# Wider load runs, a new token order and a new step order in a fused attention and channel-mix kernel

## The chip, the cores and the metric

The kernel runs on one core of one Trainium2 chip. The metric is the device time of one launch in microseconds (us), lower is better. The kernel before takes 303.88 us (median of 2 runs). Its profiled execution has a span of 301.2 us; about 2 us of launch lie between span and time. Where I speak of "fast" and "slow" runs: a run is slow when it is more than 1.5% above the fastest of its kernel, and such runs are left out.

## The reference

Eight batches of 576 tokens with 8 heads of 64. Heads 0 to 3 attend to the last 32 tokens ("plain"). Heads 4 to 7 attend to every fourth of the last 128 ("dilated"). The result is the input of a channel mix: interpolation with the token before, two matrix products with a squared ReLU between, and a sigmoid gate.

```python
mask_plain = (rel >= 0) & (rel < 32)
mask_dil   = (rel >= 0) & (rel < 128) & (rel % 4 == 0)
attn = softmax(where(mask, q @ k.T / 8, -1e9)) @ v            # (8, 8, 576, 64)
x = attn.transpose(0, 2, 1, 3).reshape(8, 576, 512)
xk, xr = mu_k * x + (1 - mu_k) * x_prev, mu_r * x + (1 - mu_r) * x_prev
out = sigmoid(xr @ w_r) * (maximum(xk @ w_k, 0)**2 @ w_v)     # (8, 576, 512), float32
```

## The kernel before

One batch's attention is cut into steps: T (transposes of q and k on TensorE, evacuated by ScalarE into `QKp` and `QKd`), S (scores, exponential, mask: `AT`), P (the product with v, then a reciprocal and a product on VectorE: `x`), X (transposes of x) and the interpolation ("lerp": `dx`, `md`, `xk`, `xr`). The channel mix ("MoE" in the code) runs in nine tiles of 512 tokens; a tile has 20 groups of 4 matmuls (8 of K, then R and V). The next batch's attention steps are placed between these groups. Engines execute in program order.

```python
    def load_qk(b, sc):                       # one token per partition, one head = 256 B
        ...
            nc.gpsimd.dma_start(out=t[:ns, w].rearrange("p (h d) -> p h d", h=H),
                                in_=src[b].transpose([1, 0, 2])[r0:r0 + ns])
    ...
    make_identity(nc, ident)
    ...
    load_batch(0)
    ...
    load_batch(1)
    ...                                       # then the loads of wk, wr, wv

    def step_T(b, sc):                        # 8 transposes of 128 columns, five such steps a batch
        ...
        nc.scalar.activation(out=QKp[b % 2][:, :, PAD + r0:PAD + r0 + ns], in_=tb[:, 0:4, 0:ns], func=AF.Copy)
        nj = ns // R
        o = QKd[b % 2][:, :, PAD:].rearrange("p a (r j) -> p a r j", r=R)[:, :, :, r0 // R:r0 // R + nj]
        nc.scalar.activation(out=o, in_=tb[:, 4:8, 0:ns].rearrange("p a (j r) -> p a r j", r=R), func=AF.Copy)
    ...
    def step_K(tt, f):
        ...
        nc.scalar.activation(out=kr, in_=pk, func=AF.Relu, scale=8.0)
        nc.vector.tensor_tensor(out=k2_of[tt][:, f], in0=kr, in1=kr, op=ALU.mult)
    ...
        for i in range(NB):                   # attn_plan: what follows which MoE group
            at(2 * i, lambda i=i: step_S(b, i))
            at(2 * i + 2, lambda i=i: step_P(b, i, 0))
            at(2 * i + 3, lambda i=i: step_P(b, i, 1))
            at(2 * i + 4, lambda i=i: step_X(b, i))
        at(15, lambda: step_lerp_d(b))
        at(16, lambda: step_lerp(b, 0))
        at(18, lambda: step_lerp(b, 1))
        ...                                   # step_T(b + 1, sc) at 4 * sc + 1
        for tt in range(NTT):
            if tt + 2 < B:
                load_batch(tt + 2)
            plan = attn_plan(tt + 1)
            for g, f in enumerate(moe_groups(tt)):
                f()
                for a in plan.get(g, []):
                    a()
```

`tb`, the PSUM tile behind T and X, has one buffer.

The softmax here doesn't subtract the row's maximum and nothing guards it: scores larger than these inputs give would overflow.

## Time and profile before

The page of the kernel before shows busy tenths in 40 slices of 7.5 us:

```profile
span 301.2 us, 5488 instructions
PE 234.5 (78%) x2000; PEld 123.6 (41%) x2000; DVE 195.0 (65%) x520; ACT 163.1 (54%) x333; POOL 160.1 (53%) x227
PE   1413553598998899789978987898889789999993
DMA  9999999999999999959995999581101201202222
q0 software_dynamic: 126336, 18.10, 86.9%
```

The DMA row looks like a bound for 200 us. But a busy queue bounds only if someone waits for it. TensorE's timeline (start, us, operation, count, and in brackets its idle time before and what ended that) says where tiles begin; these are the first K matmuls of tiles 0, 1, 2 and 5:

```profile
53.80 1.86 PE L249 MATMUL mm<-xk,wk 128*128 128x512 f16 x4 [3.50 <-DVE xk L237]
87.52 1.02 PE L249 MATMUL mm<-xk,wk 128*128 128x512 f16 x4 [0.26 <-DVE xk L237]
116.85 1.02 PE L249 MATMUL mm<-xk,wk 128*128 128x512 f16 x4 [0.54 <-DVE xk L237]
205.61 1.03 PE L249 MATMUL mm<-xk,wk 128*128 128x512 f16 x4
```

All nine: 53.8, 87.5, 116.9, 147.0, 176.2, 205.6, 234.5, 261.8, 279.2. Tiles take about 29.4 us whether loads are under way or not (the tile from 205.6 has almost none: 28.9), and 17.4 us without attention. What TensorE waits for inside a tile, from the same view:

```profile
154.92 0.26 PE L207 MATMUL tb<-ident,x_2058 96*128 96x96 f16 x2 [0.61 <-DVE x_2058 L195]
158.30 0.33 PE L207 MATMUL tb<-ident,x_2110 96*128 96x96 f16 x4 [0.31 <-ACT QKd_94 L159]
181.43 0.30 PE L188 MATMUL xo<-VA_96,AT_97 128*128 128x65 f16 x4 [1.62 <-DVE AT_97 L180]
```

No load is among them. Waits for loads are at the start only: 5.0 and 1.1 us for batch 0 itself, 8.1 and 1.2 us for batch 1's q and k near 24 us, 2.2 us for batch 2's near 60.

### The profile page before, as it was taken

How to read it: one execution, taken by the hardware profiler on the slowest of the kernel's cores; microseconds unless marked ns; L12 is line 12 of the kernel's file. 1: busy time of each engine (PE TensorE's matmuls, PEld its weight loads, DVE VectorE, ACT ScalarE, POOL GpSimd, SP SyncE). 2: the span in 40 equal slices, each digit the busy share in tenths (PEclk: the TensorE clock that was granted, in tenths of full speed). 3: DMA queues.
4: the chain of work that ended last, by engine and by line, in shares of the span. 5: the costliest groups of instructions: out<-in, count | busy, mean ns of one | idle time of the engine just before them, and what ended most of it. 6: DMA issues, size and time to landing. Idle time of an engine off the chain costs nothing.

```text
span 301.2 us, 5488 instructions
## 1 busy us (share of the span) xinstructions
PE 234.5 (78%) x2000; PEld 123.6 (41%) x2000; DVE 195.0 (65%) x520; ACT 163.1 (54%) x333; POOL 160.1 (53%) x227
## 2 busy tenths in 40 slices
PE   1413553598998899789978987898889789999993
PEld 0302342145444454445445434544454344444441
DVE  2007545946598669866986697669766976872421
ACT  1512553267647754675477557756874475352530
POOL 8999995989989999457744774440000000000000
PEclk9999999999999999999999999999999999999998
DMA  9999999999999999959995999581101201202222
GB/s 65 123 71 112 102 92 203 178 111 72 147 172 115 144 134 140 129 37 115 162 89 38 114 153 98 37 113 39 33 24 50 70 2 35 70 37 77 64 57 85
DMA packets 133052, 27.91 MB, mean 93 GB/s; under 512 B 126368, under 2 KB 127904, under 8 KB 133024
## 3 DMA queue, kind: packets, MB, share of 16 engines
q0 software_dynamic: 126336, 18.10, 86.9%
q1 hardware_dynamic: 6688, 9.45, 10.4%
q8 instruction: 16, 0.26, 0.4%
q14 instruction: 12, 0.10, 0.1%
HBM read 36.18 MB, written 9.44 MB: 151 GB/s over the span
## 4 chain that ended last, share of the span: by engine, by line
PE 32%; DVE 12%; ACT 5%; issue 2%; DVEq 0%
PE mm L269 11%; PE mm L249 9%; PE mm L258 4%; DVE md L229 3%; PE tb L207 2%; ACT kr L252 2%; PE ps L171 2%; PE xo L188 2%; DVE ot L273 2%; DVE xk L237 1%; DVE xr L237 1%; ACT QKd_94 L159 1%; PE tb L154 1%; ACT QKp_92 L156 1%; DVE AT_97 L180 1%
## 5 line engine op out<-in xcount | busy, mean ns | idle before, releaser
L249 PE MATMUL mm<-xk,wk 128*128 128x512 f16 x288 | 74.2, 390 | 5.2 <-DVE xk L237 5.2
L252 ACT ACTIVATE kr<-mm 128x512 f16<-128x512 f32 x72 | 42.7, 597 | 38.3 <-PE mm L249 30.3
L261 ACT ACTIVATE sg<-mm 128x512 f32<-128x512 f32 x36 | 21.5, 598 | 32.0 <-PE mm L258 16.5
L249 PEld LDWEIGHTS <-wk 128*128 128x128 f16 x288 | 25.2, 99 | 31.8 <-issue 4.2
L258 PE MATMUL mm<-wr,xr 128*128 128x512 f16 x144 | 37.0, 379 | 0.0
L273 DVE SCALAR_TENSOR_TENSOR ot<-sg,mm 128x512 f32<-128x512 f32 x36 | 24.6, 684 | 19.0 <-PE mm L269 19.0
L210 ACT ACTIVATE xT<-tb 128x192 f16<-128x192 f16 x48 | 15.9, 331 | 20.9 <-PE tb L207 20.9
L83 POOL DMA_DIRECT2D VA_96<-in_v_dram x36 | 23.5, 657 | 6.1 <-PE xo L188 5.6
L83 POOL DMA_DIRECT2D VA_95<-in_v_dram x36 | 24.5, 701 | 4.1 <-PE xo L188 3.2
L77 POOL DMA_DIRECT2D VA_96<-in_v_dram x24 | 18.0, 752 | 15.6 <-PE ps L171 13.9
L77 POOL DMA_DIRECT2D VA_95<-in_v_dram x24 | 18.9, 788 | 9.1 <-PE ps L171 7.5
L229 DVE TENSOR_SCALAR md<-dx,mu 128x576 f16<-128x576 f16 x64 | 22.6, 414 | 0.0
L156 ACT ACTIVATE QKp_92<-tb 128x512 f16<-128x512 f16 (+1 forms) x20 | 11.1, 552 | 18.5 <-PE tb L154 18.5
L156 ACT ACTIVATE QKp_91<-tb 128x512 f16<-128x512 f16 (+1 forms) x20 | 11.1, 553 | 17.4 <-PE tb L154 17.4
L258 PEld LDWEIGHTS <-xr 128*128 128x128 f16 x144 | 12.7, 98 | 12.6
L219 DVE TENSOR_TENSOR dx<-xT 128x1728 f16<-128x1728 f16 x8 | 8.5, 1058 | 11.9 <-ACT xT L212 11.9
L212 ACT ACTIVATE xT<-tb 128x192 f16<-128x192 f16 x48 | 15.6, 324 | 0.0
L177 ACT ACTIVATE AT_98<-ps 128x768 f16<-128x768 f32 x16 | 13.0, 814 | 4.3 <-PE ps L171 4.1
L188 PEld LDWEIGHTS <-AT_97 128*128 128x128 f16 x128 | 7.5, 103 | 18.1 <-DVE AT_97 L180 12.8
L180 DVE TENSOR_TENSOR AT_99<-AT_99,mk_177 128x768 f16<-128x768 f16 x16 | 8.9, 558 | 8.3 <-ACT AT_99 L177 8.3
L128 DVE COPY mk_168<-m_153 128x96 f16<-128x96 f16 x8 | 1.6, 400 | 19.6 <-POOL m_153 L116 19.6
L180 DVE TENSOR_TENSOR AT_98<-AT_98,mk_168 128x768 f16<-128x768 f16 x16 | 8.9, 557 | 6.7 <-ACT AT_98 L177 6.7
(532 smaller groups left out, 529.9 us busy)
## 6 DMA issues: line engine op xcount, KB each, us to landing
out_dram<-ot SPq DMA_DIRECT2D x8, 256.0 KB, 2.4
VA_95<-in_v_dram POOLq DMA_DIRECT2D x28, 64.0 KB, 3.1
VA_96<-in_v_dram POOLq DMA_DIRECT2D x28, 64.0 KB, 3.1
out_dram<-ot SPq DMA_DIRECT2D x8, 224.0 KB, 2.4
out_dram<-ot SPq DMA_DIRECT2D x8, 192.0 KB, 2.4
out_dram<-ot SPq DMA_DIRECT2D x8, 160.0 KB, 2.5
wk<-in_moe_w_k_dram POOLq DMA_DIRECT2D x4, 256.0 KB, 6.1
wv<-in_moe_w_v_dram POOLq DMA_DIRECT2D x8, 128.0 KB, 4.9
```

The lines of the kernel that those rows point to most:

```text
L77: nc.gpsimd.dma_start(out=va[row:128, i, 0:4, 0:D], in_=v[b].transpose([1, 0, 2])[lo:hi, 0:4, :])
L83: nc.gpsimd.dma_start(out=va[row:row + n, i, 4:8, 0:D], in_=vr[r, j:j + n, 4:8, :])
L156: nc.scalar.activation(out=QKp[b % 2][:, :, PAD + r0:PAD + r0 + ns], in_=tb[:, 0:4, 0:ns], func=AF.Copy)
L180: nc.vector.tensor_tensor(out=at[:, :, :, 0:QB], in0=at[:, :, :, 0:QB], in1=MK[combos[i]], op=ALU.mult)
L210: nc.scalar.activation(out=xT[:, 0:2].rearrange("p c (r j) -> p c r j", r=R)[:, :, :, nj * i:nj * (i + 1)], in_=tb[:, 0:2, 0:QB].rearrange ...
L229: nc.vector.tensor_scalar(out=md[:, c], in0=dx[:, c], scalar1=mu[:, w, c:c + 1], scalar2=None, op0=ALU.mult)
L249: nc.tensor.matmul(out=pk, lhsT=wk[:, c, f * 128:(f + 1) * 128], rhs=xk_t[tt][:, c], start=(c == 0), stop=(c == 3))
L252: nc.scalar.activation(out=kr, in_=pk, func=AF.Relu, scale=8.0)
L258: nc.tensor.matmul(out=pr, lhsT=xr_t[tt][:, c, ts * 128:(ts + 1) * 128], rhs=wr[:, c], start=(c == 0), stop=(c == 3))
L261: nc.scalar.activation(out=sg, in_=pr, func=AF.Tanh, scale=0.5)
L269: nc.tensor.matmul(out=pv, lhsT=k2_of[tt][:, f, ts * 128:(ts + 1) * 128], rhs=wv[:, f], start=(f == 0), stop=(f == 7))
L273: nc.vector.scalar_tensor_tensor(out=ot, in0=sg_of.pop((tt, ts)), scalar=1.0, in1=pv, op0=ALU.add, op1=ALU.mult)
```

## The change

Its intent is fewer and longer DMA runs. q and k come in 1-KB runs of four tokens per partition (512 B once cast to fp16); dilated v in 512-B runs; the 32 v rows that neighbouring blocks share are copied by VectorE (`fix_v`) instead of loaded twice. This changes the token order, so T makes 96 small transposes instead of 40. Weights are loaded ahead of batch 1, and tile 0 is run without waiting for batch 1. The core of the diff:

```diff
+            nc.gpsimd.dma_start(out=t[:nj, w], in_=src[b].rearrange("h (j r) d -> j h (r d)", r=R)[j0:j0 + nj])
 ...
+    load_batch(0)
     make_identity(nc, ident)
 ...
-    load_batch(1)
     ...                                      # loads of wk, wr, wv
+    load_batch(1)
 ...                                          # step_T, plain heads: 8 blocks, 96 or 48 columns each
+                    for par in range(2):
+                        nc.tensor.transpose(out=tv[par * D:(par + 1) * D, wi, sl, :],
+                                            in_=t[:nj, w, 2 * hp + par, r * D:(r + 1) * D], identity=ident[:nj, :nj])
+                o = QKp[b % 2][:, w, :, PAD:].rearrange("p h (j r) -> p h r j", r=R)[:, :, :, j0:j0 + nj]
+                nc.scalar.activation(out=o, in_=tv[:, wi].rearrange("p (h r) x -> p h r x", h=2), func=AF.Copy)
 ...                                          # step_X for two blocks at once; md as one two-tensor product
+            for n, g in enumerate((5, 9, 13, 15, 17, 18)):
+                at(g, lambda n=n: step_T(b + 1, n))
+            at(19, lambda: fix_v(b + 1))
 ...
-        plan = attn_plan(0)                  # with T of batch 1 in it
-        for g in range(20): ...
+        for i in range(NB):
+            step_S(0, i); step_P(0, i, 0); step_P(0, i, 1)      # X after every second i
+        ...
+            if tt == 0:
+                plan = {}
 ...                                          # tile 0 alone, then:
+            if tt == 0:
+                for n in range(6):
+                    step_T(1, n)
+                fix_v(1)
+                plan = attn_plan(1)          # attention 1 alone
```

More of the change, by code (lines that the diff above doesn't have):

```diff
@@ L41 @@
     const = ctx.enter_context(tc.tile_pool(name="const", bufs=1))
-    ldp = ctx.enter_context(tc.tile_pool(name="ldp", bufs=10))
+    ldp = ctx.enter_context(tc.tile_pool(name="ldp", bufs=4))
     xp = ctx.enter_context(tc.tile_pool(name="xp", bufs=2))
     xtp = ctx.enter_context(tc.tile_pool(name="xtp", bufs=2))
-    lerp_p = ctx.enter_context(tc.tile_pool(name="lerp_p", bufs=2))
+    lerp_p = ctx.enter_context(tc.tile_pool(name="lerp_p", bufs=1))
     xkp = ctx.enter_context(tc.tile_pool(name="xkp", bufs=3))
@@ L53 @@
     p_tb = ctx.enter_context(tc.tile_pool(name="p_tb", bufs=1, space=PS))
-    QKp = [const.tile([128, 4, PAD + S], FP16, name=f"QKp{i}") for i in range(2)]
-    QKd = [const.tile([128, 4, PAD + S], FP16, name=f"QKd{i}") for i in range(2)]
-    VA = [const.tile([128, NB, H, D + 1], FP16, name=f"VA{i}") for i in range(2)]
+    QKp = [const.tile([128, 2, 2, PAD + S], FP16, name=f"QKp{i}") for i in range(2)]
+    QKd = [const.tile([128, 2, 4, PAD + S // 2], FP16, name=f"QKd{i}") for i in range(2)]
@@ L59, with load_qk @@
+    VAp = [const.tile([128, NB, 4, D + 1], FP16, name=f"VAp{i}") for i in range(2)]
+    VAd = [const.tile([128, NB // 2, 4 * (2 * D + 1) + 1], FP16, name=f"VAd{i}") for i in range(2)]
     AT = [const.tile([128, 2, 4, 128], FP16, name=f"AT{i}") for i in range(3)]
+    JC = ((0, 96), (96, 48))
     ld = {}
-    def load_qk(b, sc):
-        ns = min(128, S - sc * 128)
-        r0 = sc * 128
-        t = ldp.tile([128, 2, DM], FP16, name="qk16")
+    def load_qk(b, jc):
+        j0, nj = JC[jc]
+        t = ldp.tile([96, 2, H, R * D], FP16, name="qk16")
@@ L67, in load_qk @@
         for w, src in ((0, q), (1, k)):
-            nc.gpsimd.dma_start(out=t[:ns, w].rearrange("p (h d) -> p h d", h=H),
-                                in_=src[b].transpose([1, 0, 2])[r0:r0 + ns])
-        ld[(b, sc)] = t
-    def load_v(b, i):
-        va = VA[b % 2]
-        lo = max(0, QB * i - PAD)
-        hi = QB * (i + 1)
-        row = lo - (QB * i - PAD)
-        nc.gpsimd.dma_start(out=va[row:128, i, 0:4, 0:D], in_=v[b].transpose([1, 0, 2])[lo:hi, 0:4, :])
-        vr = v[b].rearrange("h (j r) d -> r j h d", r=R)
-        while lo < hi:
-            r, j = divmod(lo, J)
-            n = min(hi - lo, J - j)
-            row = lo - (QB * i - PAD)
-            nc.gpsimd.dma_start(out=va[row:row + n, i, 4:8, 0:D], in_=vr[r, j:j + n, 4:8, :])
-            lo += n
+            nc.gpsimd.dma_start(out=t[:nj, w], in_=src[b].rearrange("h (j r) d -> j h (r d)", r=R)[j0:j0 + nj])
@@ new lines, in load_qk, with load_v @@
+        ld[(b, jc)] = t
+    def load_v(b):
+        vp, vd = VAp[b % 2], VAd[b % 2]
+        for h in range(4):
+            nc.gpsimd.dma_start(out=vp[PAD:128, :, h, 0:D], in_=v[b, h].rearrange("(i p) d -> p i d", p=QB))
+        vr = v[b, 4:8].rearrange("h (j a r) d -> a j h (r d)", a=2, r=2)
+        for i in range(3):
+            lo, hi = QB * i, QB * (i + 1)
+            while lo < hi:
+                a, j = divmod(lo, J)
+                n = min(hi - lo, J - j)
+                row = PAD + lo - QB * i
+                nc.gpsimd.dma_start(
+                    out=vd[row:row + n, i, 1:].rearrange("p (h x) -> p h x", h=4)[:, :, 0:2 * D],
+                    in_=vr[a, j:j + n])
+                lo += n
@@ L86, in load_batch, with fix_v @@
+    def fix_v(b):
+        vp, vd = VAp[b % 2], VAd[b % 2]
+        nc.vector.tensor_copy(out=vp[0:PAD, 1:NB].rearrange("p i h x -> p i (h x)"),
+                              in_=vp[QB:128, 0:NB - 1].rearrange("p i h x -> p i (h x)"))
+        nc.vector.tensor_copy(out=vd[0:PAD, 1:3], in_=vd[QB:128, 0:2])
     def load_batch(b):
-        for sc in range(5):
-            load_qk(b, sc)
-        for i in range(NB):
-            load_v(b, i)
+        for jc in range(2):
+            load_qk(b, jc)
+        load_v(b)
@@ L92 @@
     ident = const.tile([128, 128], FP16)
+    load_batch(0)
     make_identity(nc, ident)
     for i in range(2):
-        nc.vector.memset(QKp[i][:, :, 0:PAD], 0.0)
-        nc.vector.memset(QKd[i][:, :, 0:PAD], 0.0)
-        nc.vector.memset(VA[i][0:PAD, 0], 0.0)
-        nc.vector.memset(VA[i][:, :, :, D:D + 1], 1.0)
+        nc.vector.memset(QKp[i][:, :, :, 0:PAD], 0.0)
+        nc.vector.memset(QKd[i][:, :, :, 0:PAD], 0.0)
+        nc.vector.memset(VAp[i][0:PAD, 0], 0.0)
+        nc.vector.memset(VAd[i][0:PAD, 0], 0.0)
+        nc.vector.memset(VAp[i][:, :, :, D:D + 1], 1.0)
+        nc.vector.memset(VAd[i][:, :, 0:4 * (2 * D + 1) + 1:2 * D + 1], 1.0)
@@ L99 @@
     for i in range(3):
         nc.vector.memset(AT[i][:, :, :, QB:128], 0.0)
-    load_batch(0)
     wk = const.tile([128, 4, DFF], FP16, name="wk")
@@ L109 @@
     nc.vector.tensor_scalar(out=mu, in0=mu, scalar1=-1.0, scalar2=None, op0=ALU.add)
+    ones = const.tile([128, S], FP16, name="ones")
+    nc.vector.memset(ones, 1.0)
+    murep = const.tile([128, 2, 4, S], FP16, name="murep")
+    for w in range(2):
+        for c in range(4):
+            nc.scalar.activation(out=murep[:, w, c], in_=ones, func=AF.Copy, scale=mu[:, w, c:c + 1])
     m01 = const.tile([128, 3, QB], FP16, name="m01")
@@ L123 @@
     MK = {}
-    for combo in ((START, START), (FULL, MID), (FULL, FULL), (FULL, START)):
+    for combo in ((START, START), (FULL, START), (FULL, MID), (FULL, FULL)):
         t = const.tile([128, 2, 4, QB], FP16, name=f"mk{combo[0]}{combo[1]}")
@@ L129 @@
         MK[combo] = t
-    combos = [(START, START), (FULL, MID), (FULL, FULL), (FULL, START), (FULL, MID), (FULL, FULL)]
-    load_batch(1)
+    combos = [(START, START), (FULL, START), (FULL, MID), (FULL, MID), (FULL, FULL), (FULL, FULL)]
     for c in range(4):
@@ L142, in scale_wv @@
             nc.vector.tensor_scalar(out=wv[:, c], in0=wv[:, c], scalar1=1.0 / 128.0, scalar2=None, op0=ALU.mult)
-    def step_T(b, sc):
-        ns = min(128, S - sc * 128)
-        r0 = sc * 128
-        t = ld.pop((b, sc))
-        tb = p_tb.tile([128, 8, 128], FP16, name="tb")
-        for g in range(2):
-            for w in range(2):
-                for hp in range(2):
-                    c = g * 2 + hp
-                    nc.tensor.transpose(out=tb[:, g * 4 + w * 2 + hp, 0:ns],
-                                        in_=t[:ns, w, c * 128:(c + 1) * 128], identity=ident[:ns, :ns])
-        nc.scalar.activation(out=QKp[b % 2][:, :, PAD + r0:PAD + r0 + ns], in_=tb[:, 0:4, 0:ns], func=AF.Copy)
-        nj = ns // R
-        o = QKd[b % 2][:, :, PAD:].rearrange("p a (r j) -> p a r j", r=R)[:, :, :, r0 // R:r0 // R + nj]
-        nc.scalar.activation(out=o, in_=tb[:, 4:8, 0:ns].rearrange("p a (j r) -> p a r j", r=R), func=AF.Copy)
+    T_STEPS = ((0, 0, 0), (0, 0, 1), (0, 1, 0), (0, 1, 1), (1, 0, None), (1, 1, None))
@@ new lines, in step_T @@
+    def step_T(b, n):
+        jc, g, w1 = T_STEPS[n]
+        j0, nj = JC[jc]
+        t = ld[(b, jc)]
+        tb = p_tb.tile([128, 768], FP16, name="tb")
+        ws = (0, 1) if w1 is None else (w1,)
+        nw = len(ws)
+        tv = tb.rearrange("p (w s x) -> p w s x", w=nw, s=8)
+        for wi, w in enumerate(ws):
+            for sl in range(8):
+                if g == 0:
+                    hp, r = sl // 4, sl % 4
+                    for par in range(2):
+                        nc.tensor.transpose(out=tv[par * D:(par + 1) * D, wi, sl, :],
+                                            in_=t[:nj, w, 2 * hp + par, r * D:(r + 1) * D], identity=ident[:nj, :nj])
+                else:
+                    h, rp = sl // 2, sl % 2
+                    nc.tensor.transpose(out=tv[:, wi, sl, :], in_=t[:nj, w, 4 + h, rp * 2 * D:(rp + 1) * 2 * D],
+                                        identity=ident[:nj, :nj])
+        if g == 0:
+            for wi, w in enumerate(ws):
+                o = QKp[b % 2][:, w, :, PAD:].rearrange("p h (j r) -> p h r j", r=R)[:, :, :, j0:j0 + nj]
+                nc.scalar.activation(out=o, in_=tv[:, wi].rearrange("p (h r) x -> p h r x", h=2), func=AF.Copy)
+        else:
+            for wi, w in enumerate(ws):
+                o = QKd[b % 2][:, w, :, PAD:].rearrange("p h (a j) -> p h a j", a=2)[:, :, :, j0:j0 + nj]
+                nc.scalar.activation(out=o, in_=tv[:, wi].rearrange("p (h a) x -> p h a x", h=4), func=AF.Copy)
@@ L166, in step_S @@
         for sl in range(4):
-            g, hp = sl // 2, sl % 2
-            QK = (QKp, QKd)[g][b % 2]
             for par in range(2):
                 ho = par * 64
-                nc.tensor.matmul(out=ps[:, par, sl * QB:(sl + 1) * QB],
-                                 lhsT=QK[ho:ho + 64, 2 + hp, QB * i:QB * i + 128],
-                                 rhs=QK[ho:ho + 64, hp, PAD + QB * i:PAD + QB * (i + 1)],
-                                 start=True, stop=True)
+                if sl < 2:
+                    lhsT = QKp[b % 2][ho:ho + 64, 1, sl, QB * i:QB * i + 128]
+                    rhs = QKp[b % 2][ho:ho + 64, 0, sl, PAD + QB * i:PAD + QB * (i + 1)]
+                else:
+                    h, ii = 2 * (i % 2) + sl - 2, i // 2
+                    lhsT = QKd[b % 2][ho:ho + 64, 1, h, QB * ii:QB * ii + 128]
+                    rhs = QKd[b % 2][ho:ho + 64, 0, h, PAD + QB * ii:PAD + QB * (ii + 1)]
+                nc.tensor.matmul(out=ps[:, par, sl * QB:(sl + 1) * QB], lhsT=lhsT, rhs=rhs, start=True, stop=True)
         at = AT[at_n[0] % 3]
@@ L184, in step_P, with step_X @@
         at = at_of[(b, i)]
-        va = VA[b % 2]
-        xo = p_xo.tile([128, 4, D + 1], FP32, name="xo")
-        for hl in range(4):
-            nc.tensor.matmul(out=xo[:, hl], lhsT=at[:, hl % 2, g * 2 + hl // 2, :], rhs=va[:, i, g * 4 + hl, :],
-                             start=True, stop=True)
         rec = xp.tile([128, 4], FP32, name=f"rec{g}")
-        nc.vector.reciprocal(out=rec[:QB], in_=xo[:QB, :, D])
+        x16 = xp.tile([128, 4, D], FP16, name=f"x16{g}", bufs=4)
+        xo_of[(b, i, g)] = x16
         if g == 0:
-            xo_of[(b, i)] = xp.tile([128, H, D], FP16, name="x16")
-        x16 = xo_of[(b, i)]
-        nc.vector.tensor_tensor(out=x16[:QB, g * 4:g * 4 + 4, :], in0=xo[:QB, :, 0:D],
-                                in1=rec[:QB].unsqueeze(2).to_broadcast([QB, 4, D]), op=ALU.mult)
+            xo = p_xo.tile([128, 4, D + 1], FP32, name="xo")
+            for hl in range(4):
+                nc.tensor.matmul(out=xo[:, hl], lhsT=at[:, hl % 2, hl // 2, :], rhs=VAp[b % 2][:, i, hl, :],
+                                 start=True, stop=True)
+            nc.vector.reciprocal(out=rec[:QB], in_=xo[:QB, :, D])
+            nc.vector.tensor_tensor(out=x16[:QB], in0=xo[:QB, :, 0:D],
+                                    in1=rec[:QB].unsqueeze(2).to_broadcast([QB, 4, D]), op=ALU.mult)
+        else:
+            xo = p_xo.tile([128, 2, 2 * D + 2], FP32, name="xo")
+            for hl in range(2):
+                for par in range(2):
+                    o = (2 * (i % 2) + hl) * (2 * D + 1) + par * (D + 1)
+                    nc.tensor.matmul(out=xo[:, hl, par * (D + 1):(par + 1) * (D + 1)], lhsT=at[:, par, 2 + hl, :],
+                                     rhs=VAd[b % 2][:, i // 2, o:o + D + 1], start=True, stop=True)
+            rv = rec.rearrange("p (h a) -> p h a", h=2)
+            nc.vector.reciprocal(out=rv[:QB], in_=xo[:QB, :, 0:2 * D + 2:2 * D + 1])
+            nc.vector.tensor_tensor(out=x16[:QB].rearrange("p (a h) d -> p h a d", a=2),
+                                    in0=xo[:QB, :, 1:2 * D + 1].rearrange("p h (a d) -> p h a d", a=2),
+                                    in1=rv[:QB].unsqueeze(3).to_broadcast([QB, 2, 2, D]), op=ALU.mult)
     xT_of = {}
-    def step_X(b, i):
-        x16 = xo_of.pop((b, i))
+    def step_X(b, ii):
         if b not in xT_of:
@@ L204, in step_X @@
         xT = xT_of[b]
-        tb = p_tb.tile([128, 8, 128], FP16, name="tb")
-        for c in range(4):
-            nc.tensor.transpose(out=tb[:, c, 0:QB], in_=x16[:QB].rearrange("p h d -> p (h d)")[:, c * 128:(c + 1) * 128],
-                                identity=ident[:QB, :QB])
-        nj = QB // R
-        nc.scalar.activation(out=xT[:, 0:2].rearrange("p c (r j) -> p c r j", r=R)[:, :, :, nj * i:nj * (i + 1)],
-                             in_=tb[:, 0:2, 0:QB].rearrange("p c (j r) -> p c r j", r=R), func=AF.Copy)
-        nc.scalar.activation(out=xT[:, 2:4, QB * i:QB * (i + 1)], in_=tb[:, 2:4, 0:QB], func=AF.Copy)
+        tb = p_tb.tile([128, 768], FP16, name="tb")
+        tv = tb.rearrange("p (g c x) -> p g c x", g=2, c=2)
+        for u in range(2):
+            x0 = xo_of.pop((b, 2 * ii + u, 0)).rearrange("p h d -> p (h d)")
+            x1 = xo_of.pop((b, 2 * ii + u, 1)).rearrange("p h d -> p (h d)")
+            for c in range(2):
+                nc.tensor.transpose(out=tv[:, 0, c, u * QB:(u + 1) * QB], in_=x0[:QB, c * 128:(c + 1) * 128],
+                                    identity=ident[:QB, :QB])
+                nc.tensor.transpose(out=tv[:, 1, u, c * QB:(c + 1) * QB], in_=x1[:QB, c * 128:(c + 1) * 128],
+                                    identity=ident[:QB, :QB])
+        nj = 2 * QB // R
+        nc.scalar.activation(out=xT[:, 0:2].rearrange("p c (r j) -> p c r j", r=R)[:, :, :, nj * ii:nj * (ii + 1)],
+                             in_=tv[:, 0].rearrange("p c (j r) -> p c r j", r=R), func=AF.Copy)
+        lo, hi = QB * ii, QB * (ii + 1)
+        while lo < hi:
+            a, j = divmod(lo, J)
+            n = min(hi - lo, J - j)
+            o = lo - QB * ii
+            nc.scalar.activation(
+                out=xT[:, 2:4].rearrange("p c (a r j) -> p c a r j", a=2, r=2)[:, :, a, :, j:j + n],
+                in_=tv[:, 1].rearrange("p c (r x) -> p c r x", r=2)[:, :, :, o:o + n], func=AF.Copy)
+            lo += n
     xk_t, xr_t = {}, {}
@@ L227, in step_lerp @@
         md = lerp_p.tile([128, 4, S], FP16, name="md")
-        for c in range(4):
-            nc.vector.tensor_scalar(out=md[:, c], in0=dx[:, c], scalar1=mu[:, w, c:c + 1], scalar2=None, op0=ALU.mult)
+        nc.vector.tensor_tensor(out=md, in0=dx, in1=murep[:, w], op=ALU.mult)
         d = (xk_t, xr_t)[w]
@@ L301, in attn_plan @@
             at(2 * i + 3, lambda i=i: step_P(b, i, 1))
-            at(2 * i + 4, lambda i=i: step_X(b, i))
+            if i % 2 == 1:
+                at(2 * i + 4, lambda i=i: step_X(b, i // 2))
         at(15, lambda: step_lerp_d(b))
@@ L306, in attn_plan @@
         if b + 1 < B:
-            for sc in range(5):
-                at(4 * sc + 1, lambda sc=sc: step_T(b + 1, sc))
+            for n, g in enumerate((5, 9, 13, 15, 17, 18)):
+                at(g, lambda n=n: step_T(b + 1, n))
+            at(19, lambda: fix_v(b + 1))
         return plan
     with tc.manual_schedule(engines={ET.PE, ET.Activation, ET.DVE, ET.Pool}):
-        for sc in range(5):
-            step_T(0, sc)
-        plan = attn_plan(0)
-        for g in range(20):
-            for f in plan.get(g, []):
-                f()
+        for n in range(6):
+            step_T(0, n)
+        fix_v(0)
+        for i in range(NB):
+            step_S(0, i)
+            step_P(0, i, 0)
+            step_P(0, i, 1)
+            if i % 2 == 1:
+                step_X(0, i // 2)
+        step_lerp_d(0)
+        step_lerp(0, 0)
+        step_lerp(0, 1)
         scale_wv()
@@ L321 @@
                 load_batch(tt + 2)
+            gs = moe_groups(tt)
             plan = attn_plan(tt + 1)
-            for g, f in enumerate(moe_groups(tt)):
+            if tt == 0:
+                plan = {}
+            for g, f in enumerate(gs):
                 f()
@@ L326 @@
                     a()
+            if tt == 0:
+                for n in range(6):
+                    step_T(1, n)
+                fix_v(1)
+                plan = attn_plan(1)
+                for g in range(20):
+                    for a in plan.get(g, []):
+                        a()
 _INS = ['q', 'k', 'v', 'moe_mu_k', 'moe_mu_r', 'moe_w_k', 'moe_w_v', 'moe_w_r']
```

## The prediction

> **What bounds it now.** Not the loads, except at the start. The table of windows shows TensorE busy 7.5 to 9.5 us of every 10 from 60 us on; loads end near 205 us, and tiles before and after take the same time. TensorE's timeline gives the first K matmul of each MoE tile at 53.8, 87.5, 116.9, 147.0, 176.2, 205.6, 234.5, 261.8, 279.2 us: start-up 53.8, tile 0 33.7 (late loads, cold clock), about 29.3 per tile with attention interleaved, 27.2 for the last such, 17.4 for tiles 7 and 8 alone. So an interleaved attention costs about 12 us, 4 of it TensorE waiting (AT mask 1.1 to 1.6, x 0.6 twice, QKd 0.3 three times, xk 0.2 to 0.7).
>
> **The loads.** Software-queue packets fall from 126,336 to about 50,000 (estimate from the shapes), GpSimd issues from 216 to 112 (about 0.7 us each). The real waits this removes are few: 9.3 us for batch 1's q, k, 2.1 for batch 2's, and GpSimd's late mask (DVE idle 19.6 us until 23.4). The skill's "DMA: Bandwidth & Descriptors", section "Specifications", asks for 512 B or more; before has 126,368 packets under that.
>
> **What the reordering costs.** In the instruction order all of MoE 0 comes before batch 1's transposes, and attention 0 and 1 have no MoE between their steps. That gives up the overlap of one whole attention.
>
> - Start-up: the identity comes behind 12 load issues, so transposes start near 10 us instead of 5. Six transpose steps with one PSUM buffer take about 12 us (estimate: 96 transposes at 70 ns cold, evacuations of 0.8 us for 768 columns). Attention 0 in strict S, P, P, X order: the trace's chain (S 0.54, exp 0.85, mask 0.6, P to P 1.13, P to next 0.33) gives 3.45 us a block, 4.4 with X: 23.6. Then xT, dx, md, xk 5.5. First K at about 51.6.
> - Tile 0 alone: 17.4 plus 2.5 of cold clock.
> - Attention 1 alone: transposes 11.5, first mask 2, three pairs of blocks at 7 us, X(2) and the last transposes 8: about 41.
> - Tiles 1 to 5: transposes go from 40 to 96 a batch; at 40 ns instead of 54 that is 3.8 us instead of 2.1. Fewer X waits save about 2; DVE's V copy (1.3) lengthens the AT wait to about 2.2. About 29.5 each; tile 1 plus 2 for a cold clock. Tile 6 25.5.
> - md as one op: 2304 columns at dx's 0.61 ns is 1.4 us, against 1.2 to 1.8 for four: nothing.
>
> Four 512-column matmuls take 1.86 us at 54 us and 1.02 from 63 on, at the page's same granted clock. The skill's "TensorE: Matmul & The Clock Gate", Part 1, gives half rate until some 3.4 us of sustained activity; I expect attention 1 alone to fall back to it.
>
> **Sum:** 51.6 + 20 + 41 + 31.5 + 4x29.5 + 25.5 + 34.8 + 4.7 tail, plus 2.7 between span and time: about 328 us. Allowing for a faster steady tile I say 326, range 314 to 336. Faster by over 2%: 4%; within 2%: 6%; slower by over 2%: 90%.
>
> **What will show it.** Right: first K of tile 0 near 50, of tile 1 near 110, with 40 us of TensorE half idle from about 71; DMA busy share falling by half; steady tiles within 1.5 us of before. Wrong: a steady tile near 26, or attention 1 under 30 us.
>
> **What would make it wrong.** Transposes to 64 rows running two at once; waits between steps vanishing, so tiles drop to the TensorE sum of about 26.6; the clock staying at full rate in attention 1.

(The terms of the sum add up to 329.8, not to "about 328"; a slip of addition.)

## The result, and the profile after

The changed kernel takes 353.39 us (353.36 and 353.43), against 303.88. The ratio is 1.163 (95% interval 1.152 to 1.174). Ratios here are the mean time of one kernel's fast runs over that of the other's fast runs of the same rounds, so they are not quite the ratios of the medians quoted. The direction was predicted; the time lies 17 us above the range.

The page after (slices of 8.8 us):

```profile
span 351.4 us, 6171 instructions
PE 247.3 (70%) x2448; PEld 130.9 (37%) x2448; DVE 202.7 (58%) x493; ACT 190.5 (54%) x285; POOL 76.4 (22%) x123
PE   0134435973444697978788788878877977999994
PEclk9999999996555589999999999999999999999999
DMA  8999996033705920795099019904710120111312
q0 software_dynamic: 49920, 16.78, 49.0%
```

The loads did what they were meant to do: 49,920 packets instead of 126,336, and 49% of the DMA engines' time instead of 87%. TensorE has a trough of five slices in the first third, at half the granted clock. First matmuls of tile 0, of the transposes of batch 1, and of tiles 1, 4 and 5:

```profile
57.07 8.73 PE L304 MATMUL mm<-xk,wk 128*128 128x512 f16 x32 [5.27 <-DVE xk L292]
76.08 0.53 PE L175 MATMUL tb<-ident,qk 96*64 96x96 f16 x16
119.47 1.89 PE L304 MATMUL mm<-xk,wk 128*128 128x512 f16 x4
219.21 1.03 PE L304 MATMUL mm<-xk,wk 128*128 128x512 f16 x4
251.84 1.03 PE L304 MATMUL mm<-xk,wk 128*128 128x512 f16 x4
```

The stretches of the three (us of the span; before and after from the two traces):

| Stretch | before | predicted | after |
|---|---|---|---|
| start to first K | 53.8 | 51.6 | 57.1 |
| tile 0 (before: with attention 1) | 33.7 | 20 | 19.0 |
| attention 1 alone | – | 41 | 43.4 |
| tile 1 | 29.3 | 31.5 | 34.5 |
| tiles 2 to 5 | 117.7 | 118 | 130.5 |
| tile 6 | 27.2 | 25.5 | 27.2 |
| tiles 7, 8 and the end | 39.4 | 39.5 | 39.7 |

A little over half of the 24 us that the prediction missed lies in tiles 2 to 5: 32.6 us each instead of 29.5. TensorE's waits in the tile that starts at 219.21:

```profile
223.15 0.30 PE L222 MATMUL xo<-VAp,AT 128*128 128x65 f16 x4 [0.81 <-DVE AT L211]
230.49 0.20 PE L253 MATMUL tb<-ident,x 96*128 96x96 f16 x1 [1.00 <-ACT QKp L184]
234.15 0.30 PE L222 MATMUL xo<-VAp,AT 128*128 128x65 f16 x4 [0.79 <-DVE x L237]
238.25 0.20 PE L253 MATMUL tb<-ident,x 96*128 96x96 f16 x1 [1.00 <-ACT QKp L184]
250.48 0.56 PE L179 MATMUL tb<-ident,qk 48*128 48x48 f16 x16 [1.01 <-ACT QKp L184]
```

Three waits of 1.0 us for `QKp`, the evacuation of the plain heads, are new. ScalarE's groups after, with shapes kept apart (busy us and mean ns behind the bar):

```profile
L184 ACT ACTIVATE QKp<-tb 128x768 f16<-128x768 f16 x16 | 30.0, 1873 | 12.8 <-PE tb L175 12.7
L184 ACT ACTIVATE QKp<-tb 128x384 f16<-128x384 f16 x16 | 15.1, 1075 | 3.4 <-PE tb L175 3.4
L188 ACT ACTIVATE QKd<-tb 128x768 f16<-128x768 f16 x16 | 13.0, 811 | 22.8 <-PE tb L179 22.8
```

Two evacuations of the same shape: 1.87 us for plain heads, 0.81 for dilated. The first writes every fourth element (tokens of one residue), the second writes neighbours. The kernel before wrote neighbours in both; its evacuation of 512 columns for the plain heads took 0.60 us:

```profile
L156 ACT ACTIVATE QKp_91<-tb 128x512 f16<-128x512 f16 x16 | 9.5, 596 | 16.7 <-PE tb L154 16.7
```

### The profile page after: what moved, and what is told of

It reads as the page before. It is cut to its first block, busy times and chain, and to the rows that moved or that the text cites. A ratio compares the mean times of both kernels' runs of the same rounds, so it can differ in the third digit from the quotient of the medians.

```text
span 351.4 us, 6171 instructions
## 1 busy us (share of the span) xinstructions
PE 247.3 (70%) x2448; PEld 130.9 (37%) x2448; DVE 202.7 (58%) x493; ACT 190.5 (54%) x285; POOL 76.4 (22%) x123
## 3 DMA queue, kind: packets, MB, share of 16 engines
q0 software_dynamic: 49920, 16.78, 49.0%
## 4 chain that ended last, share of the span: by engine, by line
PE 43%; ACT 27%; DVE 21%; issue 5%; DMA 2%; POOL 1%; DVEq 0%; ACTq 0%; POOLq 0%
ACT QKp L184 12%; PE mm L324 12%; PE mm L304 10%; PE mm L313 5%; ACT AT L208 5%; DVE AT L211 4%; PE tb L179 4%; DVE x L237 3%; PE xo L222 3%; PE tb L175 3%; ACT xT L258 2%; DMA qk<-in_k_dram 2%; DVE k L308 2%; PE ps L205 2%; DVE md L284 2%
## 5 line engine op out<-in xcount | busy, mean ns | idle before, releaser
L324 PE MATMUL mm<-wv,k 128*128 128x512 f16 x288 | 71.8, 380 | 0.0
L307 ACT ACTIVATE kr<-mm 128x512 f16<-128x512 f32 x72 | 43.1, 604 | 33.8 <-PE mm L304 27.2
L211 DVE TENSOR_TENSOR AT<-AT,mk 128x768 f16<-128x768 f16 x48 | 26.8, 558 | 46.9 <-ACT AT L208 46.8
L184 ACT ACTIVATE QKp<-tb 128x768 f16<-128x768 f16 (+1 forms) x32 | 45.0, 1474 | 16.2 <-PE tb L175 16.1
L208 ACT ACTIVATE AT<-ps 128x768 f16<-128x768 f32 x48 | 39.1, 814 | 24.3 <-PE ps L205 24.3
L75 POOL DMA_DIRECT2D VAp<-in_v_dram x32 | 23.1, 727 | 115.7 <-PE xo L222 114.9
L308 DVE TENSOR_TENSOR k<-kr 128x512 f16<-128x512 f16 x72 | 30.0, 425 | 18.7 <-ACT kr L307 18.1
L304 PEld LDWEIGHTS <-wk 128*128 128x128 f16 x288 | 26.1, 101 | 36.3 <-issue 10.5
L188 ACT ACTIVATE QKd<-tb 128x768 f16<-128x768 f16 (+1 forms) x32 | 20.0, 650 | 28.7 <-PE tb L179 28.7
L324 PEld LDWEIGHTS <-k 128*128 128x128 f16 x288 | 24.9, 98 | 24.6
L175 PE MATMUL tb<-ident,qk 48*64 48x48 f16 (+1 forms) x512 | 16.3, 214 | 20.3 <-POOL ident masks.py:199 13.7
L284 DVE TENSOR_TENSOR md<-dx,murep 128x2304 f16<-128x2304 f16 x16 | 21.7, 1355 | 0.3
```

Source lines behind the costliest of these rows:

```text
L175: nc.tensor.transpose(out=tv[par * D:(par + 1) * D, wi, sl, :], in_=t[:nj, w, 2 * hp + par, r * D:(r + 1) * D], identity=ident[:nj, :nj])
L184: nc.scalar.activation(out=o, in_=tv[:, wi].rearrange("p (h r) x -> p h r x", h=2), func=AF.Copy)
L208: nc.scalar.activation(out=at[:, :, :, 0:QB], in_=ps[:, :, 0:4 * QB].rearrange("p a (s x) -> p a s x", s=4), func=AF.Exp, scale=0.125)
L211: nc.vector.tensor_tensor(out=at[:, :, :, 0:QB], in0=at[:, :, :, 0:QB], in1=MK[combos[i]], op=ALU.mult)
L284: nc.vector.tensor_tensor(out=md, in0=dx, in1=murep[:, w], op=ALU.mult)
L304: nc.tensor.matmul(out=pk, lhsT=wk[:, c, f * 128:(f + 1) * 128], rhs=xk_t[tt][:, c], start=(c == 0), stop=(c == 3))
```

## The experiments

Each time is the median of 4 runs (5 for run 10, a single one for run 8), and each ratio is to the kernel before on the same chip. Where results are compared across chips: before was 302.8 to 303.4 us beside these runs, and 303.9 beside the changed kernel.

### 1. The evacuation's loop order

```diff
-  o = QKp[...].rearrange("p h (j r) -> p h r j", r=R)[:, :, :, j0:j0 + nj]
-  nc.scalar.activation(out=o, in_=tv[:, wi].rearrange("p (h r) x -> p h r x", h=2), func=AF.Copy)
+  o = QKp[...].rearrange("p h (j r) -> p h j r", r=R)[:, :, j0:j0 + nj, :]
+  nc.scalar.activation(out=o, in_=tv[:, wi].rearrange("p (h r) x -> p h x r", h=2), func=AF.Copy)
```

The same elements go to the same places; only the order changes. Now the write is contiguous and the PSUM read has the step.

> The changed kernel with one edit: the evacuation of the plain heads' transposes (QKp) loops over tokens in the order of the output, so it writes contiguously and reads PSUM with a stride, instead of writing every fourth 2-byte element. Theory A (the mis-sized term is that evacuation, 1.87 us for 768 columns where QKd takes 0.81): it falls to about 0.8 us, the three TensorE waits of 1.0 us in every tile with transposes vanish, about 3 us saved in each of tiles 1 to 5 and about 3 in each of the three transpose sets outside tiles: 24 us, so about 329 us (325 to 334). Theory B (the many small transposes and the single PSUM buffer behind them cost the time, not the form of the evacuation): over 347 us, with the evacuation no shorter.

Measured: 333.99 us, correct, ratio 1.104 to before. ScalarE's group:

```profile
L184 ACT ACTIVATE QKp<-tb 128x768 f16<-128x768 f16 x16 | 13.0, 811 | 13.7 <-PE tb L175 13.7
L184 ACT ACTIVATE QKp<-tb 128x384 f16<-128x384 f16 x16 | 7.0, 488 | 3.4 <-PE tb L175 3.4
```

1.87 became 0.81, and 19.4 us went: theory A, at the weak end of its range; theory B falls. The size was overestimated because a steady tile won 2.07 us (32.63 to 30.56), not 3, and tile 6, which has no transposes, lost 1.0 (27.2 to 28.2). Why is seen in run 3.

### 2. The order of the steps

The schedule of before (as printed above, with `step_T(0, n)` for six n and `fix_v(0)` ahead of it) in the changed kernel; loads and layout as in the change.

> The changed kernel with the schedule of before: batch 1's transposes and attention 0 interleaved, attention 1 between the groups of MoE 0. Loads and layout are those of the change. Theory A (one attention's overlap was given up): the first K matmul stays near 57 us, tile 0 with attention 1 takes about 34 instead of 19 + 43, tile 1 loses its cold start; about 324 us (319 to 330). Rival C (the new order is needed, since batch 1's q and k come too late for tile 0): TensorE waits for loads in the first 60 us and the time stays over 340 us.

Measured: 324.39 us, correct, ratio 1.072. First K at 57.6, tile 1 at 91.6, where the changed kernel has 119.5: tile 0 and attention 1 together take 34.0 us instead of 62.4.

```profile
91.59 1.03 PE L304 MATMUL mm<-xk,wk 128*128 128x512 f16 x4
```

No transpose of batch 1 waits for a load in this run, so the new order was not needed for want of data. Rival C falls.

### 3. Both edits

> Both edits together. If the two causes are separate, their savings add: 353 - 24 - 29 gives about 300 us (294 to 306), about the time of the kernel before. If they overlap, more than 310.

Measured: 310.45 us, correct, ratio 1.027 (1.018 to 1.037): outside the expected range. The two savings do not add in full (19.4 and 29.0 of 353.4 would give 305). Two lines of its TensorE timeline:

```profile
34.03 0.85 PE L175 MATMUL tb<-ident,qk 96*64 96x96 f16 x16 [3.37 <-DMA qk<-in_q_dram]
214.57 0.30 PE L222 MATMUL xo<-VAp,AT 128*128 128x65 f16 x4 [1.81 <-DVE AT L211]
```

The first is lost in this run alone: at the start, batch 1's transposes come early enough to wait 3.4 us for q, which is loaded behind the weights. A further part of the loss is in tile 1, where run 1 had gained 4.3 us and run 2 1.9, but both edits together gain 3.9; why was not looked into. The second line explains the size in run 1, whose steady tiles take the same 30.56 us with the same wait: the wait for the first `AT` mask is 1.81 us instead of 0.81. VectorE comes to that mask at its own pace, behind the interpolation, the last `ot`, the v copy and a squaring, so one of the three microseconds that the evacuation gave back in a tile is waited out there.

### 4. The order alone, in the kernel before

The kernel before with the order of the change: weights ahead of batch 1, attention 0 in strict order, tile 0 alone, attention 1 alone. Its loads, layout and evacuations are untouched.

> The kernel before (its loads, layout and evacuations) with the order of the change: weights ahead of batch 1, attention 0 alone in strict order, MoE 0 alone, then attention 1 alone. Theory A: it pays the lost overlap by itself, about 26 us: about 330 us (322 to 338), with first K near 55, some 40 us of attention 1 alone. If the order is harmless and only the new layout costs: within 10 us of 304.

Measured: 329.07 us, correct, ratio 1.087. First K at 57.3, tile 0 alone 19.2, attention 1 alone 36.3, first K of tile 1 at 112.8.

```profile
57.31 9.02 PE L249 MATMUL mm<-xk,wk 128*128 128x512 f16 x32 [5.47 <-DVE xk L237]
112.78 1.87 PE L249 MATMUL mm<-xk,wk 128*128 128x512 f16 x4 [3.99 <-DVE xk L237]
```

The order (of steps and of loads) by itself costs 26 us, with none of the new layout. Its start is not shorter than that of before (53.8): there is no wait for batch 1's q, but the first P waits for its mask until 26.5 us, against 28.2 in the kernel before.

### 5. The identity first

```diff
+    make_identity(nc, ident)
     load_batch(0)
-    make_identity(nc, ident)
```

on top of run 3.

> Both edits of the third run, and the identity made ahead of batch 0's loads as in the kernel before. The first transposes start near 8 us (when q lands) instead of 14.3. Theory D: that gains little, since batch 1's q, loaded behind the weights, lands near 34 us and TensorE already waited 3.4 us for it there; the wait grows to about 9 us and the time stays near 309 us (306 to 312). Rival: the late identity alone delays the start; 6 us gained, 303 to 305.

Measured: 309.61 us (median of the 3 fast runs, 309.5 to 311.1; the fourth was slow), correct, ratio 1.023: no gain on run 3 that is clear of the noise. The profile fell in the slow state (409 us, mean granted clock 0.62), so no times of tiles are read from it. In its first 35 us the clock shown is still 1.0, and the first 16 transposes take 0.85 us as in run 3. There the first transpose is at 6.9 us instead of 14.3, and the wait for batch 1's q is 8.4 us and ends at 34.8, where run 3 waits 3.4 us until 34.0. What is gained at one end is waited out at the other, as theory D says.

### 6. Batch 1 ahead of the weights again

Run 5 with `load_batch(1)` moved back ahead of the loads of wk, wr and wv.

> The run above, and batch 1's loads put back ahead of the weights. Theory D: the wait for batch 1's q goes, first K near 46 us instead of 55; about 301 us (298 to 304). If the weights then come late, TensorE waits for them before the first K and the time stays at 306 or more.

Measured: 303.52 us, correct, ratio 1.001 (0.997 to 1.005). First K at 47.9 us; the weights are not waited for. So four edits (the order of the steps, the order of the loads and the identity's place put back, the loop order of one evacuation swapped) take back all of the 50 us, and the new loads stay in. Whether the 6 us between run 5 and this run need the earlier identity too was not tested. Against before, this version wins 6 us at the start and 1.7 in tile 0, and loses 1.1 us in each steady tile (30.55 against about 29.4) and 1.8 in tile 6.

### 7. No loads at all, in the kernel before

```diff
-            if tt + 2 < B:
-                load_batch(tt + 2)
 ...
-        t = ld.pop((b, sc))
+        t = ld[(b % 2, sc)]
```

Its output is wrong, which doesn't matter for the time.

> The kernel before, with no loads of batches 2 to 7 (they reuse the data of batches 0 and 1, so the result is wrong on purpose). It bounds what faster loads can bring from tile 0 on. Theory A: little, for loads are off the critical path there: 2.2 us of wait in tile 0 and about 0.5 us a tile of DVE time while GpSimd issues: 297 to 301 us. Rival: the loads bound the kernel before up to 200 us, and it falls below 285.

Measured: 297.03 us, ratio 0.980 (0.976 to 0.985). Removing six of eight batches' loads altogether is worth 6 us: tile 0 takes 29.8 us instead of 33.7, later tiles 28.8 instead of about 29.4. That is about the ceiling, in this schedule, for any faster load from tile 0 on. The rival, that the loads bound the kernel up to 200 us, falls.

### 8. Probes of the written step

Run 3 with ScalarE and VectorE copies of 768 columns behind the last tile, three of each; one look (342.5 us, correct; the state of a single run is unknown, but its contiguous copy takes the 0.811 us of run 1).

```python
nc.scalar.activation(out=scr[:, 0:768],    in_=pt,  func=AF.Copy)   # L392: fp16, from PSUM
nc.scalar.activation(out=scr[:, 0:1536:2], in_=pt,  func=AF.Copy)   # L393
nc.scalar.activation(out=scr[:, 0:3072:4], in_=pt,  func=AF.Copy)   # L394
...                                                                 # L395 to L397: the same from SBUF
nc.scalar.activation(out=scw[:, 0:768],    in_=pt,  func=AF.Copy)   # L398: to fp32
nc.scalar.activation(out=scw[:, 0:1536:2], in_=pt,  func=AF.Copy)   # L399
nc.vector.tensor_copy(out=scr[:, 0:768],    in_=pt)                 # L400
nc.vector.tensor_copy(out=scr[:, 0:3072:4], in_=pt)                 # L401
```

> The third run's kernel with probes behind the last tile: ScalarE copies of 768 fp16 columns from PSUM and from SBUF, written contiguously, every second and every fourth element, the same to fp32, and two VectorE copies. If the distance between written elements makes the cost: 0.8 us contiguous and about 1.9 us at every fourth from either source, with every second between or equal. If it was the PSUM read in that loop order: all the same.

The groups by line (duration in ns, least, median, greatest):

```profile
L392 ACT ACTIVATE scr<-tb x3: 811/811/811, 304.5 to 327.9; 128x768 f16<-128x768 f16 x3
L393 ACT ACTIVATE scr<-tb x3: 1021/1021/1022, 305.4 to 328.7; 128x768 f16<-128x768 f16 x3
L394 ACT ACTIVATE scr<-tb x3: 1867/1868/1868, 306.4 to 329.8; 128x768 f16<-128x768 f16 x3
L395 ACT ACTIVATE scr<-murep x3: 842/842/842, 308.3 to 331.7; 128x768 f16<-128x768 f16 x3
L396 ACT ACTIVATE scr<-murep x3: 1055/1055/1056, 309.2 to 332.6; 128x768 f16<-128x768 f16 x3
L397 ACT ACTIVATE scr<-murep x3: 1899/1899/1900, 310.3 to 333.6; 128x768 f16<-128x768 f16 x3
L398 ACT ACTIVATE scw<-tb x3: 886/887/887, 311.9 to 335.3; 128x768 f32<-128x768 f16 x3
L399 ACT ACTIVATE scw<-tb x3: 843/844/844, 312.8 to 336.2; 128x768 f32<-128x768 f16 x3
L400 DVE COPY scr<-tb x3: 556/557/558, 313.7 to 337.1; 128x768 f16<-128x768 f16 x3
L401 DVE COPY scr<-tb x3: 1853/1854/1854, 314.3 to 337.7; 128x768 f16<-128x768 f16 x3
```

The written step makes the cost, from PSUM and from SBUF alike: 0.81 us contiguous, 1.02 at every second, 1.87 at every fourth fp16 element (0.84, 1.06 and 1.90 from SBUF). It is not the distance in bytes alone: fp32 at every second element, also 8 bytes apart, takes 0.84, no more than contiguous fp32. VectorE's copy slows from 0.56 to 1.85. In run 1 the PSUM read has the step, and the time is 0.811, that of the contiguous copy: a stepped read of PSUM costs nothing here. Why fp16 and fp32 differ stays open.

### 9. VectorE's order

Run 6, with two moves: `fix_v` in group 11 instead of 19, and each squaring (`k2`) emitted behind the attention steps of its group.

```diff
-            at(19, lambda: fix_v(b + 1))
+            at(11, lambda: fix_v(b + 1))
 ...
-        nc.vector.tensor_tensor(out=k2_of[tt][:, f], in0=kr, in1=kr, op=ALU.mult)
+        late.append(lambda: nc.vector.tensor_tensor(out=k2_of[tt][:, f], in0=kr, in1=kr, op=ALU.mult))
 ...                                  # after the steps of each group:
+                while late:
+                    late.pop(0)()
```

> The 303.5 us version (loads of the change, contiguous evacuation, interleaved attention, identity first, batch 1 ahead of the weights) with two moves in the order of VectorE only: the V copy for the next batch in group 11 instead of 19, and each squaring of MoE behind the attention steps of its group instead of ahead of them. Theory: steady tiles there wait on VectorE's order, 1.8 us for the first AT mask (of which the V copy is 0.9) and 0.7 + 0.8 us for x behind a squaring that waits for ScalarE. 1.5 to 2 us a tile for 7 tiles: about 291 us (287 to 296). If those waits are set by something else, 300 or more.

Measured: 294.95 us, correct, ratio 0.975 (0.973 to 0.978): faster than both kernels. TensorE's waits in one of its tiles:

```profile
171.20 0.30 PE L222 MATMUL xo<-VAp,AT 128*128 128x65 f16 x4 [0.49 <-DVE AT L211]
174.42 0.30 PE L222 MATMUL xo<-VAp,AT 128*128 128x65 f16 x4 [0.69 <-DVE x L237]
181.21 0.30 PE L222 MATMUL xo<-VAp,AT 128*128 128x65 f16 x4 [0.88 <-DVE x L237]
```

The time was hit for half of the reason. The `AT` wait fell from 1.81 to 0.49. The waits for `x` (0.7 and 0.8 before) did not fall: the late squaring of the group before now stood in the same place. The two moves were not run apart.

### 10. The control: the same delayed squaring in the kernel before

> The kernel before with the same delayed squaring and nothing else: the control that says how much of the version above is the order and how much the loads. It has x waits of 0.6 us twice a tile and an AT wait of 1.1 to 1.6: about 1.3 us a tile, about 294 us (291 to 299). If it is not slower than the version above, the new loads bring nothing even at their best.

Measured: 298.01 us, correct, ratio 0.985. So of run 9's gain of 8 us on before, about 5 come without any of the new loads, and run 9 is 3 us ahead of this control (two medians of the same chip).

### 11. xr's interpolation on GpSimd

```diff
-        nc.vector.tensor_tensor(...)          # both ops of step_lerp
+        (nc.vector, nc.gpsimd)[w].tensor_tensor(...)
```

on top of run 9.

> The first version with xr's two-step interpolation on GpSimd, which is idle there, instead of VectorE. Theory: xr is needed only eight groups later, so the remaining AT wait (about 1 us a tile) goes too: 283 to 289. If GpSimd's operations slow VectorE's next to them, or end too late for the R matmuls, no gain or a loss.

Measured: 346.28 us, correct, ratio 1.145: a loss of 51 us on run 9. VectorE's `md` and GpSimd's, side by side in the two engines' timelines:

```profile
192.71 5.40 DVE L284 TENSOR_TENSOR md<-dx,murep 128x2304 f16<-128x2304 f16 x1
192.35 4.54 POOL L284 TENSOR_TENSOR md<-dx,murep 128x2304 f16<-128x2304 f16 x1 [13.03 <-DVE dx L277]
```

VectorE's takes 1.36 us alone. Here it ends at 198.11, 1.22 us after GpSimd's ends at 196.89, so it hardly moved beside it. The Trainium skill's "SBUF — State Buffer", section "Who interferes with whom", states this: a VectorE instruction with two SBUF inputs contends with a GpSimd instruction that reads SBUF, and what they share is "an exclusive lock". This run agrees. TensorE then waits for `xk`, VectorE's half of the interpolation, in total, times and longest (us):

```profile
PE mm L305 <- DVE xk L292: 38.8, 8, 6.6
```

That is most of the 51 us. No matmul waits for GpSimd's `xr`, so the other cause that was expected, an `xr` that ends too late, falls.

### 12. Squarings in pairs

Run 9 with the late squarings emitted only after odd groups:

```diff
-                while late:
+                while late and (g % 2 == 1 or g > 7):
```

> The first of the three runs above (295.0 us), with the squarings emitted in pairs behind the second attention step of two groups, so that none stands between an AT mask and the x after it. There one still did (0.42 us at 173.4 of its trace), and the x waits of 0.7 and 0.9 us stayed. Theory: those two waits shrink by about 0.35 us each, 0.7 a tile for 7 tiles: about 290 us (288 to 293). If the pairs then hold up kr's two buffers, or x waits for the exponential alone, no gain: 294 to 296.

Measured: 292.02 us, correct, ratio 0.963 (0.958 to 0.968): the best version, 3.7% faster than before. The same waits:

```profile
169.55 0.30 PE L222 MATMUL xo<-VAp,AT 128*128 128x65 f16 x4 [0.50 <-DVE AT L211]
172.43 0.30 PE L222 MATMUL xo<-VAp,AT 128*128 128x65 f16 x4 [0.35 <-DVE x L237]
178.96 0.30 PE L222 MATMUL xo<-VAp,AT 128*128 128x65 f16 x4 [0.62 <-DVE x L237]
```

The waits for `x` shrank by 0.34 and 0.26 us, and tiles take 29.03 us instead of 29.62. Pairs were not tried in the kernel before, so how much of the 3.7% needs the new loads is not shown; without pairs it was 3 us of 8 (run 10).

## Why the prediction was right or wrong

- **Right: the loads are off the critical path but for the start.** With no loads after batch 1 the kernel before gains only 6 us (run 7), while the change halved the DMA engines' share.
- **Right: the order gives up the overlap of one attention.** Predicted first K of tile 1 "near 110", measured 119.5; attention 1 alone 43.4 against 41; tile 0 alone 19.0 against 20. Alone in the kernel before, the order costs 26 us (run 4); the order of the steps alone, in the changed kernel, 29 (run 2). That the 41 was so close is luck: it assumed cheap evacuations, and with the loop order swapped attention 1 takes 36.6 (run 1).
- **Right: the clock falls back.** The windows from 80 to 120 us have a granted clock of 0.50 to 0.55, and the transposes there run at half speed (those of X start 0.08 us apart in the timeline at 98 us, 0.04 apart at 133 us). The Trainium skill's "TensorE: Matmul & The Clock Gate", section "Part 4: PE-mode transpose", adds that a transpose "doesn't count as PE-busy the same way" for the gate. That fits, but no run here tests it apart from the idle time.
- **Wrong, and the main miss: "evacuations of 0.8 us for 768 columns".** This cost holds for copies that write neighbours and was applied to one that writes every fourth fp16 element. It measured 1.87. It stands behind a single PSUM buffer, so TensorE waited 1.0 us for it three times in each steady tile, where the sum (29.5, "within 1.5 us of before") has no such wait, and 2.0 us three times in each transpose set outside the tiles. The evacuation is 19 of the 24 to 27 us missed. With the loop order swapped the kernel takes 334 us, inside the predicted range; but that is partly luck, for errors of other terms cancel there: against run 1 the start and tiles 2 to 6 were too low by 10 us together, attention 1 and tiles 0 and 1 too high by 6.
- **Wrong: the steady tile without it.** Run 1 has 30.56 us a tile where I said 29.5. I counted the waits that vanish (X) and the longer `AT` wait (2.2 predicted, 1.81 in run 3), but not three waits of 0.5 to 0.8 us for `x`, which P now meets where X met it before.
- **Wrong: the identity "near 10 us".** The first transpose starts at 13.7 us. GpSimd's timeline has its last three load issues ahead of the identity waiting 1.4, 1.1 and 0.5 us for earlier loads to land. On top of run 3 making it earlier gains nothing by itself (run 5), since batch 1's q then is late; in the changed kernel itself, which does not wait for that q, it was not tried.
- **Right in size: `md` as one operation.** 1.36 us, against 1.2 to 1.8 for four.

The accounting of the 50 us: the order of steps and loads 26 (run 4 against before); the written step 19 (the changed kernel against run 1); 4 to 5 for the rest, by subtraction, which includes the longer tile and the later identity. It depends on the order of undoing: in the interleaved kernel the evacuation is worth 14 (run 2 against run 3); the wait for batch 1's q explains 3.4 us of the difference.

## What to carry to other kernels

A DMA row at 9 of 10 is not a bound: look whether a compute engine waits for a load, and if in doubt run the kernel without the loads. Price a copy by the way it writes as well as by its size: if a reorder must happen while evacuating, put the step on the side that reads (shown here for ScalarE reading PSUM). When work is taken out of an interleaved stretch to avoid one wait, the price is the whole overlap, here some 26 us to avoid waits of about 12, of which little could be had (run 4: the mask came next).

## What the Trainium skill lacked or had wrong

- "SBUF — State Buffer", section "Door 1: The DMA port swizzle (why `[64,N]` ≈ `[32,N]`)", says in its note on cachelines that one can stride for free up to 8 bf16 elements. For writes of another 16-bit type, fp16, this does not hold: a ScalarE copy of 768 columns took 0.81 us contiguous, 1.02 at every second and 1.87 at every fourth element. (A VectorE copy took 1.85 at every fourth too, but its contiguous 0.56 is faster than ScalarE's, so how much of its slowing is the step alone is not shown.) For fp32 (free up to 4 by that note) every second element was indeed free: 0.84 against 0.89.
- "ScalarE: Activation LUTs" gives no cost for a stepped output at all. A stepped read of PSUM was free (0.811 us in run 1), which no page states for ScalarE.
- "TensorE: Matmul & The Clock Gate", section "Seeing it yourself", warns in general that the trace's clock events are not to be fully trusted; it does not say that the clock shown can miss the gate at the start. Before its first warm-up the kernel ran four 512-column matmuls in 1.86 us at a shown clock of 1.00, and in 1.02 later at the same shown clock; the later cold stretch of the changed kernel does show 0.50.
